# A long convolution with a gated MLP: how the input product of the first stage is laid out, evicted and loaded

## The chip, the core and the metric

The kernel runs on one core of a Trainium2 chip. The core's engines run programs of their own and wait for each other by semaphores: PE (TensorE) multiplies matrices out of on-chip memory (SBUF) into accumulators (PSUM), DVE (VectorE), ACT (ScalarE) and POOL (GpSimd) work element by element, and SP (SyncE) mostly issues DMAs. ACT and POOL can issue DMAs too. The metric is the device time of one execution in microseconds.

## What is computed

With S = 2048 positions and D = 640 channels (the reference, cut):

```python
def _A_ref(q, k, v, shift_k, ssm_k, ssm_D):
    k_pad = jnp.pad(k, ((0, 0), (ks - 1, 0), (0, 0)))          # ks = 4
    for t in range(ks):
        k_shift = k_shift + k_pad[:, t:t + S, :] * shift_k[:, ks - 1 - t][None, None, :]
    kv = k_shift * v
    # causal convolution of kv with ssm_k over 2048 positions, per channel, by FFT of length 2S
    y = irfft(rfft(kv) * rfft(ssm_k))[:S] + kv * ssm_D
    return q * y

mod = silu(c) @ w_mod                                           # six rows: sa, ca, ga, sb, cb, gb
h = layernorm(x) * (1 + ca) + sa                                # x = A_q
x = x + ga * _A_ref(h, A_k, A_v, A_shift_k, A_ssm_k, A_ssm_D)
h = layernorm(x) * (1 + cb) + sb
x = x + gb * (relu(h @ w1 + b1) ** 2 @ w2 + b2)                 # 640 -> 1728 -> 640
```

All inputs are fp32.

## The kernel before

The long convolution is done as a Fourier transform in two steps, both as products on PE. Position s is split as s = 64 n + i: n (32 values) lies on partitions, i (64 values) in the row. The channels are worked on in five blocks b of 128, and a block's channels stand as four groups a of 32 on partitions 32 a to 32 a + 31 (n inside). Blocks 1 and 2, and 3 and 4, share their loads (s is the number of such a load group: 0, 1, 2).

- *The short convolution* (`load_kv` L853, `kv` L874). A unit (s, u) holds 1024 elements on each partition: n = 32 or 16 values of i, by 32 or 64 channels. The tile `kt` has three rows more at its front, since the tap t looks back t positions. Of unit 0 these three rows are k's rows 61 to 63 of the partition before (position 64 n - 3 and on); eight small DMAs on ACT's queue fetch them, after POOL has cleared the three rows for the first partition of each group. Of later units ACT copies them. Then DVE, and for two of the four taps in groups 0 and 1 POOL, multiply `kt`, shifted by t, with the taps; DVE adds up in PSUM (`acc`, two banks) and multiplies with v into the tiles `px`. The taps lie in the channel's order, four to a channel, so that one tap's row steps 16 bytes. `px` is kept as (channel, i), so DVE writes it in steps of 256 bytes.
- *First step* (`unit_a` L906). For input (`px`, i = 0) and filter (`ph`, i = 1) of a block: each of a block's 32 channels of a group and each half of the partitions is a stationary matrix of 64 partitions by 64 columns, against the constants `cw` as the moving one; products for two halves e and two parts r go to the four quarters of the array. The profile counts two instructions for each fp32 product: 256 for one `px` or `ph`. ACT evicts 512 elements at a time to the tile `a` (`pac`): in pairs (d) before, the two elements of a pair 128 bytes apart in `a`.
- *Second step and back* (`spectra` L928, `front` L949, `back` L977, `unit_y` L1002): products of `a` with `gb`, the spectra's product on DVE and POOL (tiles `wx`), products with `gi` into `q` (evicted by ACT in runs of eight), transposes, products with `ca`, and the gate with the normalised q (tiles `up`). `early_h` (L943) does the filter's spectra of block 0 ahead. Besides there are the six rows of `mod` (products of `wm`) and the statistics of q's rows (BN_STATS on DVE).
- Then the MLP, 8 runs of 256 tokens over 14 slices of the hidden width, with weights split in two fp32r parts that stay in SBUF.

The names in the profile are those of the memory a tile lies in: `px` and `ph` are S0p or S1p (of block 0: `px` is S0p, `ph` is S1p), `kt`, v and the taps are KV, the tap products `up`, the sums `ps`, the tiles `m` are `wx`, and the spectra of `early_h` and the q tiles XP0p and XP1p.

The order of the work is not that of the code. Each operation is a node with an engine, a cost (`cost` L640) and its buffers; a planner (`order` L216) plays the engines against each other and takes on each the first ready node by the numbers in the table `URGE`, one for each node. What it gives out is a fixed order for each engine. An engine's queue is worked off strictly in that order. A DMA on SP also waits until the one `OUT` places ahead of it has landed (`sp_issue` L616). Most lines of the profile say L402, where `emit` issues all operations; so groups are told apart by their tiles.

Of the kernel before, what the change touches and what calls it, by code (L numbers as in the profile page):

```python
# [25 lines left out]
OUT = 4  # L26
# [87 lines left out]
class Graph:  # L114
# [101 lines left out]
    def order(self, lag=0.06, pelag=0.1, phase=0.0):  # L216
# [92 lines left out]
        dma_free, landed = 0.0, []  # L309
# [95 lines left out]
def _constants():  # L405
# [17 lines left out]
    for mm in range(1, 32):  # L423
# [32 lines left out]
        "cw": np.hstack([cw, gb[:, 0, 1, 0], gx]).astype(f),  # L456
# [7 lines left out]
def ssm_mlp_kernel(  # L464
# [37 lines left out]
    ident = sb.tile([P, P], F32, tag="ident", name="ident")  # L502
# [7 lines left out]
    cst = sb.tile([P, 256], F32, tag="cst", name="cst")  # L510
# [3 lines left out]
    ca = cst[:, 192:256]  # L514
    warm = sb.tile([P, 1], F32, tag="warm", name="warm")
    nc.scalar.dma_start(cst[:, 0:192], cw_d[:, 0:192])
# [123 lines left out]
    def cost(engine, op, args, kw):  # L640
# [7 lines left out]
        if engine == "DVE":  # L648
# [6 lines left out]
            return 0.17 + 0.001 * n if op != "scalar_tensor_tensor" else 0.17 + 0.00112 * n  # L655
# [168 lines left out]
    def load_gi(i):  # L824
# [6 lines left out]
        if i == 0:  # L831
            g.key = ("lgi", 0)
            sp_dma(gi[0:64, 1, 0].rearrange("p c n -> p (c n)"), cw_d[0:64, 192:320], 512)
# [6 lines left out]
    def load_taps(first):  # L840
        g.key = ("ltap", 0)
        if first:
            src = shift_k[:P].rearrange("(a c) t -> a (c t)", a=4)
            sp_dma(tapb[:, 0:128], src.unsqueeze(1).to_broadcast([4, 32, 128]), 512)
            return
        for s in range(2):
            src = shift_k[P + 256 * s : P + 256 * s + 256].rearrange("(a c) t -> a (c t)", a=4)
            sp_dma(tapb[:, 128 + 256 * s : 384 + 256 * s], src.unsqueeze(1).to_broadcast([4, 32, 256]), 1024)
# [4 lines left out]
    def load_kv(s, u):  # L853
# [20 lines left out]
    def kv(s, u):  # L874
# [3 lines left out]
        taps = tapb[:, at : at + 4 * w].rearrange("p (c t) -> p t c", t=4)  # L878
# [3 lines left out]
        for t in range(4):  # L882
            o = sbuf(f"ktmp_{s}_{u}_{t}", (P, n, w), TMP) if t else acc
# [808 lines left out]
```

## Time and profile before

| what | value |
|---|---|
| median of 3 runs | 739.98 us (738.59 to 777.24) |
| the profiled execution | 739.45 us |
| its span, first to last instruction | 737.7 us |
| mean granted TensorE clock | 0.974 |
| PE, share of the span | 646.3 us, 88% |
| weight loads, DVE, ACT, POOL | 574.6, 452.9, 337.4, 268.7 us |
| DMA | 62.47 MB in 108155 packets |

The span is 1.75 us shorter than the execution's own time. Weight loads (PEld) run beside PE's products. An engine's busy time is spread over stages that have different limits, so the stages are read one by one. In a row of waits stand the time in total, how often, and the longest.

### The profile page before, as it was taken

The numbers are of one execution on the slowest core, as the hardware profiler recorded it, in microseconds if no ns is written. First come the engines' busy times: TensorE is split into PE (matmuls) and PEld (weight loads), VectorE is DVE, ScalarE is ACT, GpSimd is POOL, SyncE is SP. The second block draws the span as 40 slices with busy tenths as digits, with TensorE's granted clock in tenths as the row PEclk, the third lists the DMA queues.
The fourth block names the chain that finished last, engine by engine and source line by source line (L and its number), as shares of the span: only waits on it lengthen the run. The fifth ranks groups of instructions, "written<-read, shape, count | busy, mean of one in ns | idle before, by whom it ended". The sixth has DMA issues, their size and how long they took to land.

```text
span 737.7 us, 17486 instructions
## 1 busy us (share of the span) xinstructions
PE 646.3 (88%) x7401; PEld 574.6 (78%) x7401; DVE 452.9 (61%) x754; ACT 337.4 (46%) x639; POOL 268.7 (36%) x259
## 2 busy tenths in 40 slices
PE   0048798978698989989999999999999999999996
PEld 0047575867577878849999988999999999999896
DVE  1798789789997736786526437446456365464432
ACT  1157256588768798655423424324324233243220
POOL 4647470666655765843311132102103004021001
PEclk9989999988889999998999999999999999999999
DMA  8698689979607521344201011002010020020011
GB/s 113 121 180 194 160 226 234 240 176 190 151 2 150 166 85 45 111 129 129 68 1 42 32 36 36 1 1 72 1 41 33 1 72 1 1 72 1 1 37 36
DMA packets 108155, 62.47 MB, mean 85 GB/s; under 512 B 78316, under 2 KB 98220, under 8 KB 108076
## 3 DMA queue, kind: packets, MB, share of 16 engines
q1 hardware_dynamic: 101884, 58.02, 33.3%
q10 hardware_dynamic: 5936, 3.32, 2.0%
q8 instruction: 58, 0.95, 0.6%
q14 instruction: 21, 0.17, 0.1%
q0 software_dynamic: 256, 0.00, 0.0%
HBM read 52.15 MB, written 9.18 MB: 83 GB/s over the span
## 4 chain that ended last, share of the span: by engine, by line
PE 74%; DVE 7%; DMA 7%; ACT 6%; issue 3%; POOL 3%; SPq 0%; ACTq 0%; DVEq 0%; POOLq 0%
PE ps L402 74%; ACT a L402 5%; DMA KV<-in_A_k_dram 2%; DVE up L402 2%; DMA KV<-in_A_v_dram 2%; DVE ps L402 1%; POOL up L402 1%; DVE wx L402 1%; DMA wm<-in_w_mod_dram 1%; DVE mtmp L402 1%; DMA gb<-in_gb_dram 1%; DMA S1p<-in_A_ssm_k_dram 1%; POOL wx L402 0%; SPq L617 0%; ACTq L402 0%
## 5 line engine op out<-in xcount | busy, mean ns | idle before, releaser
L402 PE MATMUL ps<-xt,w_S 128*128 128x256 f32 (+1 forms) x680 | 129.3, 331 | 0.0
L402 PEld LDWEIGHTS ps<-xt,w_S 128*128 128x128 f32 x680 | 104.8, 190 | 10.3 <-DVE xfs L402 0.2
L402 ACT ACTIVATE mtmp<-ps,b1t 128x256 f32<-128x256 f32 (+1 forms) x112 | 51.4, 473 | 113.7 <-PE ps L402 108.2
L402 PE MATMUL ps<-a,gb 128*64 128x128 f32 x1260 | 82.0, 281 | 8.7 <-DVE wx L402 5.1
L402 PEld LDWEIGHTS ps<-a,gb 128*64 128x64 f32 x1260 | 71.5, 140 | 22.5 <-DVE wx L402 7.4
L402 ACT ACTIVATE a<-ps 128x512 f32<-128x512 f32 x80 | 77.3, 1105 | 20.0 <-PE ps L402 19.7
L402 DVE TENSOR_TENSOR mtmp<-ps,mtmp 128x256 f32<-128x256 f32 (+1 forms) x99 | 41.1, 419 | 69.0 <-ACT mtmp L402 68.0
L402 PE MATMUL ps<-w_S,hring 128*128 128x320 f32 x456 | 78.0, 310 | 0.0
L402 POOL TENSOR_TENSOR wx<-wx 128x256 f32<-128x256 f32 x80 | 68.1, 872 | 20.0 <-DVE wx L402 19.7
L402 PEld LDWEIGHTS ps<-w_S,hring 128*128 128x128 f32 x456 | 70.1, 188 | 1.4
L402 DVE TENSOR_TENSOR hring<-mtmp,hring 128x256 fp32r<-128x256 f32 x74 | 36.3, 496 | 53.8 <-ACT hring L402 53.8
L402 PE MATMUL ps<-cst,S0p 64*64 64x64 f32 x1024 | 24.6, 255 | 50.3 <-DMA KV<-in_A_k_dram 43.2
L402 PEld LDWEIGHTS ps<-cst,S0p 64*64 64x64 f32 x1024 | 21.9, 165 | 55.4 <-DVE S0p L402 45.7
L402 ACT ACTIVATE hring<-mtmp 128x256 fp32r<-128x256 f32 x74 | 30.6, 416 | 67.9 <-PE ps L402 51.3
L402 POOL TENSOR_TENSOR x<-x,gb2row 128x640 f32<-128x640 f32 x16 | 25.3, 1594 | 90.6 <-ACT mtmp L402 90.6
L402 DVE TENSOR_TENSOR wx<-ps,wx 128x512 f32<-128x512 f32 x64 | 40.9, 685 | 22.8 <-PE ps L402 21.8
L402 POOL TENSOR_TENSOR x<-mtmp,x 128x640 f32<-128x640 f32 (+1 forms) x9 | 13.5, 1506 | 108.0 <-DVE mtmp L402 108.0
L402 POOL TENSOR_TENSOR up<-KV 128x1024 f32<-128x1024 f32 x12 | 38.0, 3188 | 27.7 <-DVE ps L402 16.6
L402 DVE TENSOR_TENSOR up<-KV 128x1024 f32<-128x1024 f32 x18 | 43.0, 2396 | 5.3 <-DMA KV<-in_A_k_dram 4.8
L402 DVE SCALAR_TENSOR_TENSOR mtmp<-mtmp 128x256 f32<-128x256 f32 x91 | 44.9, 500 | 1.8
L402 PE MATMUL ps<-gi,wx 64*128 64x128 f32 x640 | 41.5, 278 | 4.4 <-ACT q L402 2.0
L402 ACT ACTIVATE wx<-ps 128x512 f32<-128x512 f32 x49 | 29.5, 608 | 32.3 <-PE ps L402 29.1
(156 smaller groups left out, 1318.6 us busy)
## 6 DMA issues: line engine op xcount, KB each, us to landing
wm<-in_w_mod_dram SPq DMA_DIRECT2D x25, 320.0 KB, 4.1
KV<-in_A_k_dram SPq DMA_DIRECT2D x40, 128.0 KB, 3.7
KV<-in_A_v_dram SPq DMA_DIRECT2D x40, 128.0 KB, 4.5
S1p<-in_A_ssm_k_dram SPq DMA_DIRECT2D x20, 256.0 KB, 5.3
q<-in_A_q_dram SPq DMA_DIRECT2D x8, 640.0 KB, 4.3
out_dram<-x SPq DMA_DIRECT2D x14, 320.0 KB, 3.6
w1s<-in_B_w_dram SPq DMA_DIRECT2D x13, 320.0 KB, 3.4
w2s<-in_B_w_dram SPq DMA_DIRECT2D x13, 320.0 KB, 2.9
```

Of the source, the lines that this page charges most:

```text
L402: fn(*real, **{k: a.real() if isinstance(a, View) else a for k, a in kw.items()})
```

## The change

Six things, and a new table:

1. *Taps apart.* `load_taps` loads the taps into a staging tile and ACT copies them into four rows of neighbouring channels, one for each tap. The loads go row by row as before.
2. *Evictions in runs of eight.* `pac` goes through PSUM in steps of 64 elements, so that eight neighbouring elements of `a` are written one after the other.
3. *Last rows by a product.* k's rows 61 to 63 come by four plain DMAs a group into a tile of their own (`kend`). PE multiplies them with an identity shifted by one column (`step`), which moves each partition's rows to the next; ACT evicts them with a factor of 0 for the first partition of each group and 1 elsewhere (`later`, a new column of the constants).
4. *One queue.* These loads and the second half of the loads of q (`load_xp`) go to SP; ACT's queue keeps three at the start.
5. *`px` as k and v lie*: (i, channel) instead of (channel, i). DVE writes it in one run; PE's stationary columns are 128 bytes apart.
6. *`OUT` is 6 instead of 4*, and two costs in the planner change: the first DMA is assumed 2.5 us later, and operations of 1024 elements on DVE a little dearer. The tap products now take their buffers in the order of the program.

```diff
-OUT = 4
+OUT = 6
...
-        dma_free, landed = 0.0, []
+        dma_free, landed = 2.5, []
...
-    ident = sb.tile([P, P], F32, tag="ident", name="ident")
+    step = sb.tile([P, P + 1], F32, tag="ident", name="step")
+    ident, step = step[:, 1:], step[:, 0:P]
+    nc.vector.memset(step[:, 0:1], 0.0)
...
+        raw = sbuf(f"tap_{int(first)}", (P, D), [whole(f"STG{i}") for i in range(4)])
+        for s in (0,) if first else (1, 2):
+            at, w = (0, 128, 384)[s], WIDE[s]
+            src = shift_k[at : at + 4 * w].rearrange("(a c) t -> a (c t)", a=4)
+            sp_dma(raw[:, at : at + 4 * w], src.unsqueeze(1).to_broadcast([4, 32, 4 * w]), 16 * w)
+            copy(
+                act,
+                tapb[:, at : at + 4 * w].rearrange("p (t c) -> p c t", t=4),
+                raw[:, at : at + 4 * w].rearrange("p (c t) -> p c t", t=4),
+            )
...
         if u == 0:
-            pool.memset(kt[:, 0:3], 0.0)
-        else:
-            copy(act, kt[:, 0:3], KT[s, u - 1][:, n : n + 3])
+            end = sbuf(f"kend_{s}", (P, 3, w), [part(parent("XP1", 2560), 2048, ("XP1c",))])
         for a in (0, 2, 1, 3):
             cols = slice(BASE[s] + w * a, BASE[s] + w * a + w)
             if u == 0:
-                act_dma(kt[32 * a + 1 : 32 * a + 17, 0:3], kshift[0:16, 0:3, cols], 4 * w)
-                act_dma(kt[32 * a + 17 : 32 * a + 32, 0:3], kshift[16:31, 0:3, cols], 4 * w)
+                sp_dma(end[32 * a : 32 * a + 32], ksrc[:, 61:64, cols], 4 * w)
             sp_dma(kt[32 * a : 32 * a + 32, 3:], ksrc[:, n * u : n * u + n, cols], 4 * w)
+        if u == 0:
+            t = psum(f"kend_{s}", (P, 3, w), ANY)
+            with g.as_one(0.3):
+                mm(t.rearrange("p i c -> p (i c)"), step, end.rearrange("p i c -> p (i c)"), True, True)
+            act.activation(kt[:, 0:3], t, AF.Copy, scale=later)
+        else:
+            copy(act, kt[:, 0:3], KT[s, u - 1][:, n : n + 3])
...
-        taps = tapb[:, at : at + 4 * w].rearrange("p (c t) -> p t c", t=4)
+        taps = tapb[:, at : at + 4 * w].rearrange("p (t c) -> p t c", t=4)
...
-            mul(dve, px[b][:, :, n * u : n * u + n].rearrange("p g i -> p i g"), acc[:, :, c], vt[:, :, c])
+            mul(dve, px[b][:, n * u : n * u + n], acc[:, :, c], vt[:, :, c])
...
-                                (ph if i else px)[b][l, 8 * n + j, :],
+                                ph[b][l, 8 * n + j, :] if i else px[b][l, :, 8 * n + j],
...
-            o = AX[b][i].rearrange("p m (e d g) -> p m g e d", e=2, d=2)[:, :, 8 * n : 8 * n + 8, e]
-            copy(act, o, t[e].rearrange("p g m d -> p m g d"))
+            o = AX[b][i].rearrange("p m (e d g) -> p m e d g", e=2, d=2)[:, :, e, :, 8 * n : 8 * n + 8]
+            copy(act, o, t[e].rearrange("p g m d -> p m d g"))
...
-            (act_dma if h else sp_dma)(
-                t[64 * h : 64 * h + 64], qsrc[h, :, 4 * j : 4 * j + 4, BASE[s] : BASE[s] + w], 4 * w
-            )
+            sp_dma(t[64 * h : 64 * h + 64], qsrc[h, :, 4 * j : 4 * j + 4, BASE[s] : BASE[s] + w], 4 * w)
...
     URGE = {
-        ("b1", 0): [-1209, -1601],
```

The table `URGE` is new throughout, so every engine's order changes. Three places follow. The rows give the line, the operation, the tile written, the tiles read, and the shape; x2 means twice in a row.

The first loads on SP's queue. KV<-in_A_k_dram and KV<-in_A_v_dram are k and v, KV<-in_A_shift_k_dram the taps, XP1p<-in_A_k_dram the last rows, S1p<-in_A_ssm_k_dram the filter of block 0. Before:

```order
L617 DMA KV<-in_A_shift_k_dram 128x1x256
L617 DMA KV<-in_A_k_dram 32x32x32 x2
L617 DMA KV<-in_A_shift_k_dram 128x1x256
L617 DMA KV<-in_A_v_dram 32x32x32 x2
L617 DMA KV<-in_A_shift_k_dram 128x1x128
L617 DMA KV<-in_A_k_dram 32x32x32 x4
L617 DMA KV<-in_A_v_dram 32x32x32
L617 DMA KV<-in_A_k_dram 32x32x32
L617 DMA KV<-in_A_v_dram 32x32x32
L617 DMA KV<-in_A_k_dram 32x32x32
L617 DMA gb<-in_gb_dram 128x1024
L617 DMA KV<-in_A_v_dram 32x32x32 x3
```

Now:

```order
L621 DMA gb<-in_gb_dram 128x1024
L621 DMA KV<-in_A_k_dram 32x32x32 x3
L621 DMA XP1p<-in_A_k_dram 32x3x32
L621 DMA KV<-in_A_k_dram 32x32x32 x2
L621 DMA XP1p<-in_A_k_dram 32x3x32
L621 DMA KV<-in_A_k_dram 32x32x32 x2
L621 DMA tap_122<-in_A_shift_k_dram 128x1x128
L621 DMA KV<-in_A_v_dram 32x32x32
L621 DMA XP1p<-in_A_k_dram 32x3x32
L621 DMA KV<-in_A_k_dram 32x32x32
L621 DMA S1p<-in_A_ssm_k_dram 32x32x64
L621 DMA XP1p<-in_A_k_dram 32x3x32
```

The constants gb go first, the taps in the middle, and the filter's loads begin among those of k and v instead of behind them.

PE's first products. Before, the input's (S0p) come first and, after 128 of them, the filter's (S1p):

```order
L402 MATMUL ps_91<-cst,S0p 64x64 x2
L402 MATMUL ps_95<-cst,S0p 64x64 x2
L402 MATMUL ps_90<-cst,S1p 64x64 x2
L402 MATMUL ps_92<-cst,S1p 64x64 x2
L402 MATMUL ps_90<-cst,S1p 64x64 x2
```

Now the filter's 128 come first, then spectra of it (a, gb), and then, with the last rows of group 1 (XP1p, step) ahead, the input's:

```order
L402 MATMUL ps_94<-a_0_165,gb 64x128 x8
L402 MATMUL ps_92<-a_0_165,gb 64x128 x8
L402 MATMUL ps_93<-XP1p,step 128x192
L402 MATMUL ps_91<-a_0_165,gb 64x128 x8
L402 MATMUL ps_93<-cst,S0p 64x64 x2
L402 MATMUL ps_94<-cst,S0p 64x64 x2
```

The product with `step` waits for the loads of the last rows of group 1, which are SP's DMAs 30, 33, 37 and 40, and everything behind it on PE waits with it.

DVE's first work after the vector for `mod`. Before, the two units of group 0 follow each other:

```order
L402 TENSOR_TENSOR up_132<-KV 128x1024
L402 TENSOR_TENSOR ps_96<-KV 128x1024
L402 TENSOR_TENSOR ps_96<-ps_96,up_132 128x1024 x3
L402 TENSOR_TENSOR S0p<-ps_96,KV 128x32x32
L402 TENSOR_TENSOR ps_96<-KV 128x1024
L402 TENSOR_TENSOR up_132<-KV 128x1024
```

Now the statistics of the first q rows stand inside the second unit (four such pairs of rows, the first shown):

```order
L402 TENSOR_TENSOR ps_97<-KV 128x1024
L402 TENSOR_TENSOR up_142<-KV 128x1024
L402 TENSOR_TENSOR ps_97<-ps_97,up_142 128x1024 x3
L402 TENSOR_TENSOR S0p<-ps_97,KV 128x1024
L402 TENSOR_TENSOR up_142<-KV 128x1024
L402 BN_STATS s_217<-q_148 128x6 x2
L402 BN_AGGR st_238<-s_217 128x2
```

The product into S0p now writes one run of 1024 instead of a 32 by 32 pattern, and eight BN_STATS with four BN_AGGR stand ahead of the rest of the second unit.

More of the change, by code (lines that the diff above doesn't have):

```diff
@@ L509, in ssm_mlp_kernel @@
     nc.gpsimd.memset(dsm, 0.0)
-    cst = sb.tile([P, 256], F32, tag="cst", name="cst")
+    cst = sb.tile([P, 257], F32, tag="cst", name="cst")
     cw = cst[:, 0:128].rearrange("p (r n) -> p r n", r=2)
     gbx = cst[:, 128:192]
-    ca = cst[:, 192:256]
+    ca = cst[:, 193:257]
+    later = cst[:, 192:193]
     warm = sb.tile([P, 1], F32, tag="warm", name="warm")
-    nc.scalar.dma_start(cst[:, 0:192], cw_d[:, 0:192])
+    nc.scalar.dma_start(cst[:, 0:193], cw_d[:, 0:193])
     for a in range(4):
```

196 lines of the change are left out of this document (100 added, 96 removed), and 310 rows, old and new, of the table URGE.

## Prediction

> **What bounds the kernel now.** I read the slices of the page first, then a table by stage, then who PE (TensorE) waits for, then the groups of the early stages. In the slices each digit is a fortieth of the span, 18.4 us; PEclk is the granted TensorE clock.
>
> ```profile
> span 737.7 us, 17486 instructions
> ...
> PE   0048798978698989989999999999999999999996
> ...
> PEclk9989999988889999998999999999999999999999
> ```
>
> PE is idle for two slices, then broken up for some fifteen, then full to the end. The change touches only what stands ahead of the full part. The same by stage; the columns are the length, the busy time of PE, weight loads, DVE, ACT and POOL, then the clock, DMA share and GB/s.
>
> ```profile
> 0.00:12.00 12.00, 0.00 (x0) 0.00 (x0) 0.26 (x3) 2.98 (x4) 5.40 (x17) 1.00 0.59 90
> 12.00:24.00 12.00, 0.00 (x0) 0.00 (x0) 7.32 (x3) 2.04 (x3) 5.40 (x3) 1.00 1.28 175
> 0.00:43.25 43.25, 0.00 (x1) 0.00 (x1) 21.95 (x16) 6.88 (x10) 21.37 (x24) 1.00 0.80 130
> 43.25:72.30 29.05, 23.40 (x688) 21.67 (x688) 26.87 (x20) 21.60 (x27) 17.60 (x8) 0.88 0.95 188
> 72.30:150.00 77.70, 69.67 (x1124) 53.17 (x1122) 64.56 (x99) 38.73 (x59) 37.32 (x42) 0.98 0.83 213
> 150.00:226.00 76.00, 58.52 (x1280) 49.93 (x1280) 69.44 (x70) 58.56 (x104) 47.43 (x43) 0.87 0.63 126
> 226.00:329.50 103.50, 96.45 (x1746) 75.65 (x1746) 67.96 (x104) 78.75 (x138) 65.64 (x66) 1.00 0.42 117
> 329.50:737.70 408.20, 398.30 (x2567) 374.20 (x2567) 202.07 (x450) 132.90 (x303) 79.31 (x81) 0.99 0.11 32
> ```
>
> The MLP (from 329.5) is PE's: 398.3 of 408.2 us. Ahead of it there are four stages with different limits. Until 43.25 PE has nothing to do. From 43.25 to 72.3 it lacks 5.65 us (29.05 - 23.40), from 72.3 to 150 8.0, from 150 to 226 17.5, and from 226 on 7.05. The stage from 150 to 226 is the loose one: DVE is busy for 69.4 of 76 us, ACT for 58.6, and the clock is 0.87. What PE waits for between 43 and 331 us:
>
> ```profile
> PE ps L402 <- ACT a L402: 12.7, 18, 2.1
> PE ps L402 <- DVE wx L402: 8.5, 6, 3.3
> PE ps L402 <- POOL S1p L402: 4.2, 2, 3.1
> PE ps L402 <- DVE up L402: 4.0, 3, 1.8
> ...
> PE ps L402 <- DVE S0p L402: 2.1, 2, 1.9
> ```
>
> The largest is the eviction of the first stage (tile a), then work that stands behind DVE. So ACT's evictions and DVE's queue are the two things to price.
>
> **Evictions in runs of eight.** These are the groups that carry the sum (busy us, mean ns of one):
>
> ```profile
> L402 ACT ACTIVATE a<-ps 128x512 f32<-128x512 f32 x80 | 77.3, 1105 | 20.0 <-PE ps L402 19.7
> ...
> L402 DVE TENSOR_TENSOR up<-KV 128x1024 f32<-128x1024 f32 x18 | 43.0, 2396 | 5.3 <-DMA KV<-in_A_k_dram 4.8 <-issue 0.4
> ...
> L402 DVE TENSOR_TENSOR wx<-ps,wx 128x512 f32<-128x512 f32 x64 | 40.9, 685 | 22.8 <-PE ps L402 21.8 <-POOL wx L402 0.7 <-ACT wx L402 0.3
> ...
> L402 DVE TENSOR_TENSOR ps<-ps,up 128x1024 f32<-128x1024 f32 x30 | 36.9, 1231 | 7.2 <-POOL up L402 6.1
> ...
> L402 DVE TENSOR_TENSOR ps<-KV 128x1024 f32<-128x1024 f32 x10 | 27.3, 2728 | 0.1
> ...
> L402 ACT ACTIVATE q<-ps 128x512 f32<-128x512 f32 x39 | 21.6, 601 | 16.8 <-PE ps L402 15.9 <-ACT q L402 0.8
> ...
> L402 DVE TENSOR_TENSOR S0p<-ps,KV 128x512 f32<-128x512 f32 x12 | 12.2, 1057 | 2.2 <-DMA KV<-in_A_v_dram 2.1
> ...
> L402 DVE TENSOR_TENSOR S0p<-ps,KV 128x1024 f32<-128x1024 f32 x2 | 3.9, 1937 | 0.1
> ```
>
> The eviction to q already has the pattern that the one to a gets: runs of eight elements out, steps of 64 elements in PSUM, 512 elements. It takes 601 ns against 1105. I take 601, so ACT loses 80 x 0.504 = 40.3 us. Ends: the whole 40.3, or nothing if the PSUM side is what is slow (the q row speaks against that).
>
> **Taps apart.** Single instructions, or short rows of them, on DVE and on POOL (GpSimd):
>
> ```profile
> 33.50 1.97 DVE L402 TENSOR_TENSOR ps<-KV 128x1024 f32<-128x1024 f32 x1
> ```
> ```profile
> 163.64 1.28 DVE L402 TENSOR_TENSOR up<-up,row 128x512 f32<-128x512 f32 x2
> ```
> ```profile
> 18.54 4.64 DVE L402 TENSOR_TENSOR ps<-KV 128x1024 f32<-128x1024 f32 x1
> ```
> ```profile
> 16.67 4.67 POOL L402 TENSOR_TENSOR up<-KV 128x1024 f32<-128x1024 f32 x1 [3.94 <-DMA KV<-in_A_k_dram]
> ```
> ```profile
> 69.18 2.95 POOL L402 TENSOR_TENSOR up<-KV 128x1024 f32<-128x1024 f32 x1
> ```
> ```profile
> 72.32 3.46 POOL L402 TENSOR_TENSOR wx<-wx 128x256 f32<-128x256 f32 x5
> ```
>
> A tap product alone (taps 16 bytes apart) takes 1.97 us for 1024 elements. Two products of 512 with contiguous operands take 1.28, so 1024 take about 1.25: 0.72 less. DVE does 18 + 10 = 28 of them: 20 us. That they average 2.4 and 2.7 is another cost: the product at 18.54 took 4.64 us beside POOL's at 16.67, so the two block each other, and a shorter one blocks for less; I put nothing on that. The product with v goes from scattered to contiguous output: 16 x (1.06 - 0.685), with the tile wx as model, and 2 x (1.94 - 1.23) make 7.4 us. So DVE loses 27.5 us. POOL's 12 products take 2.95 us alone; its contiguous rows take 3.46 / 5 = 0.69 for 256 elements, 2.8 for 1024. So POOL gains nothing.
>
> **Last rows by a product, and one queue.** Twenty-four small DMAs leave ACT's queue, as do 12 loads of q, and three memsets leave POOL. Where they were late they held up DVE ahead of 43.25, which is reckoned anew below; behind it no row above names them, so I count no gain. SP gets 12 loads of k's last rows and the 12 of q, PE three products, ACT three scaled copies and three for the taps: about 1 us on the path. What is new is a wait: in PE's queue the product of the last rows of the second group stands ahead of the first input product (tile S0p), and it needs the fortieth DMA that SP issues. Sizes of the transfers:
>
> ```profile
> KV<-in_A_k_dram SPq DMA_DIRECT2D x40, 128.0 KB, 3.7
> ...
> S1p<-in_A_ssm_k_dram SPq DMA_DIRECT2D x20, 256.0 KB, 5.3
> ...
> gb<-in_gb_dram SPq DMA_DIRECT2D x2, 512.0 KB, 5.0
> ```
>
> **The start.** Before, PE starts with S0p, which waits for two whole units of DVE. Now it starts with S1p (the filter). Ahead of and with the fourth S1p load SP issues 3.52 MB: gb 0.52, k 1.05, last rows 0.05, taps 0.33, v 0.52, S1p 1.05. At 90 GB/s for 12 us and then 175 (first two stage rows) these land at 12 + 2.44 / 0.175 = 26 us; the first filter product follows, 17 us sooner. Up to the fortieth DMA come v 0.52, q 1.31, w_mod 0.33, gi 0.52, gb 0.52, k 0.39 and last rows 0.10 more, 7.2 MB in all: 12 + 6.15 / 0.175 = 47 us, and S0p cannot go on PE before. DVE is no later: it starts when k and the taps are in, near 16 us (1.8 MB by the same rates), and has four tap products, six sums, two products with v and q's first statistics to do until then. Rates of PE's products, and one row of DVE:
>
> ```profile
> 153.24 2.19 PE L402 MATMUL ps<-cst,S1p 64*64 64x64 f32 x128 [0.57 <-ACT wx L402]
> ```
> ```profile
> 252.34 4.59 PE L402 MATMUL ps<-a,gb 128*64 128x128 f32 x80
> ```
> ```profile
> L402 DVE BATCH_NORM_STATS2 s<-q 128x6 f32<-128x320 f32 x32 | 14.2, 475 | 0.4 <-DMA q<-in_A_q_dram 0.4
> ```
>
> The eight statistics moved ahead cost DVE 8 x 0.475 = 4 us; with 4 x 1.25 + 6 x 1.23 + 2 x 1.23 = 15 us that is 19, or 35 us from the start, and some 12 us of POOL's products may block it: covered by the 47, and gone as cover if the loads are faster. PE takes 17 ns for a small product, 57 for a large one. By 72.3 PE had done 512 small and 176 large. In the new order 256 small and 112 large stand ahead of S0p (11 us, done by about 40 with cold clock and waits). Behind it, up to the same total, 256 small and 64 large remain: 4.4 + 3.7 = 8 us, with a part at a low clock 10. That makes 57 against 72.3: **15 us** gained. Ends: 8 (loads no faster than 130 GB/s, the row up to 43.25) and 22 (six in flight reach the 213 of the row to 150).
>
> **The loose stages.** From 72.3 to 150 PE lacks only 8.0 us, and DVE loses 9 there (some eight products and eight with v): **5 us**, ends 0 and 10. (Less than the 9, since PE itself is nearly full.) From 150 to 226 alone:
>
> ```profile
> L402 ACT ACTIVATE a<-ps 128x512 f32<-128x512 f32 x24 | 23.5, 1103 | 2.8 <-PE ps L402 2.7
> ```
> ```profile
> L402 DVE TENSOR_TENSOR up<-KV 128x1024 f32<-128x1024 f32 x9 | 23.2, 2581 | 0.5 <-issue 0.4
> ...
> L402 DVE TENSOR_TENSOR ps<-KV 128x1024 f32<-128x1024 f32 x3 | 6.2, 2050 | 0.0
> ```
>
> Twelve tap products and six with v fall here: 12 x 0.72 + 6 x 0.38 = 11 us off DVE, and 24 evictions take 12 us off ACT. PE lacks 17.5 and loses up to 10 more by its clock (0.13 x 76). DVE is full there, so its 11 us count in full, and 2 for the clock: **13 us**, ends 5 and 24. From 226 on 24 evictions are left, and only waits for them go: **3 us**, ends 0 and 6. The MLP does not move.
>
> **Stationary columns at a stride.** The input's 1280 weight loads now read columns 128 bytes apart. No weight load of before does that over more than 8 bytes. The nearest row is the tap product: 1.97 for 1.25 where each element is 16 bytes from the last, a factor of 1.58. Were a small product wholly its load, 17 ns would become 27: 1280 x 10 = 13 us. But four quarters of the array work in turn, and part of the 17 ns is the product itself, so I take half, **6 us lost**; ends 0 and 22 (all doubled).
> SBUF — State Buffer (section Door 1: The DMA port swizzle, the note on cachelines) in the Trainium skill says that the memory's lines are 16 bytes, that each access to a new line pays, and that one may step four fp32 for free. It speaks against this part of the change. The trace agrees for DVE that new lines pay (1.97 against 1.25 us), though its taps are just four fp32 apart, which the page calls free. Taken in full for the weight loads, this is rival 2.
>
> **Sum.** On the profiled execution's 739.45 us (span 737.7; 0.5 under the median 739.98): 739.45 - 15 - 5 - 13 - 3 + 6 + 1 = 710 us.
>
> **Rivals.**
> 1. *Strided weight loads decide, and it is slower.* The gains are 36 us and the small costs 1, so at 35 / 1280 = 27 ns more on each input product nothing is left, and at 39 ns more (56 instead of 17) it is slower by 2%. If a load costs four times as much and the quarters don't overlap, it is 1280 x 51 = 65 us: 769. For it: no row shows such loads. Against: every strided row here costs less than twice.
> 2. *Strided loads cost their factor in full.* 13 us instead of 6: 717. For it: the tap row. Against: the quarters overlap, and PE has slack in the loose stage.
> 3. *Loads set the pace.* Until 226 us PE and DVE use 37 MB (130 x 43 + 188 x 29 + 213 x 78 + 126 x 76). If six in flight bring no more, the stages from 72.3 on gain 11 instead of 21: 720. For it: DMA shares of 0.95 and 0.83. Against: 0.63 in the loose stage.
> 4. *It unlocks more.* If PE runs nearly full from 26 us, the upper ends hold (22 + 10 + 24 + 6 = 62) and the stride costs 4: 739 - 62 + 5 = 682.
> 5. *The change does not do what it says.* Evictions stay at 1105 ns because reading PSUM in steps is what is slow: the start gains 8, the two stages behind it 5 each, the last none, and the stride costs 13: 739 - 18 + 14 = 735. For it: nothing but the risk; the q row is against it.
>
> **How the numbers follow.** Two per cent, about what a measurement of this kernel can tell from no change, is 725 to 755. Chances: the forecast (698 to 714) 0.40, rival 4 (below 698) 0.18, rival 2 (714 to 719) 0.12, rival 3 (719 to 725) 0.10, rival 5 and its like (725 to 755) 0.12, rival 1 0.08. So faster 0.80, same 0.12, slower 0.08. I leave out 0.07 at the fast end and 0.11 at the slow end: 685 to 728.
>
> **What would show it.** Groups: a<-ps near 600 ns; tap products near 1.3 us where POOL rests; the product with v near 0.69. The start: first S1p product near 26 us, first S0p product near 47 with PE waiting for k's last rows. Stride: 64 input products in more than 1.09 us (17 ns each). Xt, the MLP's first product, near 300 instead of 329.5. I am wrong if the input products take over 40 ns, if DVE waits for k or v again and again, or if the first MLP product comes at 320 or later.

## The result and the profile after

| kernel | median | against before on the same chip, 95% interval |
|---|---|---|
| before | 739.87 us | 1 |
| changed | 744.22 us (743.52 to 745.25, 4 runs) | 1.0066 (1.0045 to 1.0086) |

The changed kernel is 5 us slower (0.45 to 0.86 per cent); 710 was forecast. The ratio is of fast runs alone, and one run of before, of 777 us, was slow. The page of the changed kernel's profile shows PE starting a slice sooner and full no sooner:

```profile
span 742.8 us, 17442 instructions
...
PE   0298699877589999968999999999999999999996
...
PEclk9998899989899999987999999999999999999999
...
q8 instruction: 58, 0.95, 0.6%
```

By stretches (length, busy time of PE, weight loads, DVE, ACT, POOL, clock, DMA share, GB/s), cut where the first product of the transform (filter or input) and where the MLP's first product begin. Before, from 43.25 on (the stretch ahead of it stands in the prediction):

```profile
43.25:329.55 286.30, 248.04 (x4834) 200.46 (x4835) 228.88 (x290) 197.69 (x328) 168.05 (x156) 0.95 0.64 152
329.55:737.70 408.15, 398.30 (x2567) 374.17 (x2567) 202.02 (x450) 132.85 (x303) 79.27 (x81) 0.99 0.11 32
```

After:

```profile
0.00:28.90 28.90, 0.71 (x2) 0.50 (x2) 8.80 (x11) 7.41 (x11) 12.47 (x21) 1.00 1.02 152
28.90:336.96 308.06, 264.75 (x4840) 219.48 (x4841) 218.64 (x304) 172.49 (x339) 167.86 (x159) 0.94 0.67 152
336.96:742.80 405.84, 396.81 (x2565) 373.31 (x2565) 197.54 (x441) 128.64 (x296) 75.58 (x78) 0.99 0.10 28
```

Read as a ledger of spans: PE starts 14.4 us sooner. Then it is busy 16.7 us longer (264.75 - 248.04), and idle 5.1 longer (43.3 against 38.3). The MLP gives 2.3 back. That makes +5.1, with DVE 10 us and ACT 25 us less busy in the middle stretch. The groups after, and two of them before:

```profile
L402 ACT ACTIVATE a<-ps 128x512 f32<-128x512 f32 x80 | 42.6, 599 | 37.1 <-PE ps L402 37.1
...
L402 PE MATMUL ps<-cst,S0p 64*64 64x64 f32 x1024 | 35.3, 288 | 3.1 <-issue 3.1
...
L402 DVE TENSOR_TENSOR up<-KV 128x1024 f32<-128x1024 f32 x18 | 26.3, 1465 | 4.0 <-ACT KV L402 3.9
...
L402 DVE TENSOR_TENSOR ps<-KV 128x1024 f32<-128x1024 f32 x10 | 15.7, 1571 | 7.7 <-DMA KV<-in_A_k_dram 7.7
L402 DVE TENSOR_TENSOR S0p<-ps,KV 128x512 f32<-128x512 f32 x12 | 8.0, 685 | 2.4 <-PE ps L402 2.2
L402 DVE TENSOR_TENSOR xt<-xfs,xt 128x256 fp32r<-128x256 f32 x5 | 5.4, 1105 | 0.0
```

```profile
L402 PE MATMUL ps<-cst,S0p 64*64 64x64 f32 x1024 | 24.6, 255 | 50.3 <-DMA KV<-in_A_k_dram 43.2 <-ACT a L402 3.9 <-DVE S0p L402 2.1
L402 DVE TENSOR_TENSOR xt<-xfs,xt 128x256 fp32r<-128x256 f32 x5 | 3.1, 634 | 0.4 <-ACT xt L402 0.4
```

Evictions, taps and products with v came out as forecast or nearly so. The input products (S0p; 1024 of the 1280, one block lies elsewhere) cost PE 10.7 us more (35.3 against 24.6); the other 6 of the 16.7 are small rises in many groups, the largest that of the spectra's products (a, gb: 86.0 us against 82.0), at a granted clock of 0.94 against 0.95. What PE waits for from 20 us on (10.3 of POOL S1p is the wait at the start):

```profile
PE ps L402 <- issue: 13.1, 7, 4.4
PE ps L402 <- DVE wx L402: 12.1, 7, 5.1
PE ps L402 <- POOL S1p L402: 11.2, 2, 10.3
PE ps L402 <- ACT a L402: 4.5, 4, 2.2
PE ps L402 <- DVE xfs L402: 4.4, 1, 4.4
PE ps L402 <- ACT mtmp L402: 4.0, 2, 3.2
```

The wait for a fell from 12.7 to 4.5, as the evictions promised. New are 13.1 us of "issue" (2.2 before: PE waits for nothing that the profile shows), 3.6 more for wx, and 8.4 at the entry of the MLP. PE and then DVE there:

```profile
324.21 1.07 PE L402 MATMUL ps<-wx,cst 128*64 128x512 f32 x2
328.50 2.81 PE L402 MATMUL ps<-step,mtmp 128*128 128x128 f32 x11 [3.22 <-ACT mtmp L402]
332.10 0.47 PE L402 MATMUL ps<-step,mtmp 128*128 128x128 f32 x1 [0.79 <-ACT mtmp L402]
336.96 2.90 PE L402 MATMUL ps<-xt,w_S1a 128*128 128x256 f32 x12 [4.39 <-DVE xfs L402]
```

```profile
328.07 2.90 DVE L402 TENSOR_TENSOR w_S<-w2s,w_S 128x640 fp32r<-128x640 f32 x2
330.89 0.53 DVE L402 TENSOR_SCALAR xfs<-ps,cbs 128x256 f32<-128x256 f32 x1
331.34 1.54 DVE L402 TENSOR_TENSOR w_S<-w1s,w_S 128x640 fp32r<-128x640 f32 x2
332.81 3.43 DVE L402 TENSOR_TENSOR xt<-xfs,xt 128x256 fp32r<-128x256 f32 x2
336.27 0.54 DVE L402 TENSOR_SCALAR xfs<-ps,cbs 128x256 f32<-128x256 f32 x1
```

PE's last product of the convolution ends at 325.3, and PE comes to the MLP at 337 (before at 326.6 and 329.55). In the new order DVE's subtractions for weights stand ahead of xt, and xt takes 1.7 us each beside POOL's additions.

Three theories came of this. A: the strided columns double the product, and that ate the gains. B: six transfers in flight hold up PE's instructions (the issue waits). D: what ACT and DVE saved was never on the path.

### The profile page after: what moved, and what is told of

It is laid out like the page before. It is cut to its first block, busy times and chain, and to the rows that moved or that the text cites. A ratio compares the mean times of both kernels' runs of the same rounds, so it can differ in the third digit from the quotient of the medians.

```text
span 742.8 us, 17442 instructions
## 1 busy us (share of the span) xinstructions
PE 662.3 (89%) x7407; PEld 593.3 (80%) x7407; DVE 425.0 (57%) x755; ACT 308.5 (42%) x645; POOL 255.9 (34%) x256
## 4 chain that ended last, share of the span: by engine, by line
PE 80%; DVE 7%; DMA 6%; issue 3%; ACT 2%; SPq 1%; POOL 1%; DVEq 0%; POOLq 0%; ACTq 0%
PE ps L402 80%; DVE up L402 2%; DMA KV<-in_A_k_dram 2%; DVE wx L402 1%; DMA KV<-in_A_v_dram 1%; DMA S1p<-in_A_ssm_k_dram 1%; SPq L621 1%; DMA XP0p<-in_A_q_dram 1%; DVE ps L402 1%; DVE mtmp L402 1%; ACT a L402 1%; DMA XP1p<-in_A_k_dram 1%; ACT up L402 0%; DMA wm<-in_w_mod_dram 0%; DVE xt L402 0%
## 5 line engine op out<-in xcount | busy, mean ns | idle before, releaser
L402 PE MATMUL ps<-a,gb 128*64 128x128 f32 x1260 | 86.0, 288 | 14.5 <-DVE wx L402 7.9
L402 PEld LDWEIGHTS ps<-a,gb 128*64 128x64 f32 x1260 | 74.5, 144 | 27.2 <-DVE wx L402 10.8
L402 DVE TENSOR_TENSOR hring<-mtmp,hring 128x256 fp32r<-128x256 f32 x74 | 39.3, 540 | 64.9 <-ACT hring L402 61.3
L402 POOL TENSOR_TENSOR wx<-wx 128x256 f32<-128x256 f32 x80 | 64.2, 819 | 34.4 <-DVE wx L402 33.8
L402 ACT ACTIVATE a<-ps 128x512 f32<-128x512 f32 x80 | 42.6, 599 | 37.1 <-PE ps L402 37.1
L402 POOL TENSOR_TENSOR x<-mtmp,x 128x640 f32<-128x640 f32 (+1 forms) x9 | 13.1, 1464 | 123.9 <-DVE mtmp L402 123.9
L402 PE MATMUL ps<-cst,S1p 64*64 64x64 f32 x1536 | 32.4, 237 | 20.1 <-POOL S1p L402 11.2
L402 PEld LDWEIGHTS ps<-cst,S1p 64*64 64x64 f32 x1536 | 29.9, 154 | 22.8 <-POOL S1p L402 11.6
L402 PE MATMUL ps<-xt,w_S1a 128*128 128x256 f32 (+1 forms) x170 | 38.2, 343 | 6.0 <-DVE xfs L402 4.4
L402 PE MATMUL ps<-gi,wx 64*128 64x128 f32 x640 | 43.2, 286 | 0.1
L402 PEld LDWEIGHTS ps<-gi,wx 64*128 64x128 f32 x640 | 39.4, 195 | 4.6 <-issue 3.7
```

The lines of the kernel that those rows point to most:

```text
L402: fn(*real, **{k: a.real() if isinstance(a, View) else a for k, a in kw.items()})
```

## Experiments on the changed kernel

All ratios below are to runs of before on the same chip, with 95% intervals. One per cent is 7.4 us. Each trace shows one execution.

**The stride.** e1 undoes part 5, e9 stores px in pairs of channels, and e3 has another distance in each block (DVE's product with v and PE's stationary operand follow the layout; those lines are left out here):

```diff
-        px[b] = sbuf(f"px_{b}", (P, 64, DG), HALF[:3], line="px")
+        px[b] = sbuf(f"px_{b}", (P, DG, 64), HALF[:3], line="px")             # e1
+        px[b] = sbuf(f"px_{b}", (P, DG // 2, 64, 2), HALF[:3], line="px")     # e9
+        px[b] = sbuf(f"px_{b}", (P, DG // (1, 2, 4, 8, 16)[b], 64, (1, 2, 4, 8, 16)[b]), HALF[:3], line="px")     # e3
```

> The changed kernel with px laid out as before (channel, i), so that the stationary columns are neighbours again and DVE writes px in steps of 256 bytes; order unchanged. Theory A (the strided columns double the input product, 1280 x 15 to 17 ns = 19 to 22 us, and that is what ate the gains): 64 input products in 1.1 us again, 720 to 728 us. Rival D (what ACT and DVE saved was never on the path, and the stride isn't either): 738 to 746. Rival B (six DMAs in flight hold up PE's instructions): PE's waits put down to issue stay near 13 us, 735 to 742.

> The changed kernel with another layout of px in each block: stationary columns 4 bytes apart in block 0, 8 in block 1, 16 in block 2, 32 in block 3, 64 in block 4. It asks what the cost of a stride depends on: 64 input products take 1.1 us at 4 bytes and 2.1 to 2.2 at 128. If lines of 16 bytes decide: under 1.6 us at 8 bytes, 2.1 from 16 bytes on. If any step between columns costs the same: 2.1 at 8 bytes already. If the cost grows with the step: under 1.5 at 16 bytes. Time by theory A between the two layouts: 730 to 740 us.

> The changed kernel with px in pairs of channels (columns 8 bytes apart), nothing else. Theory F (PE's instructions are the floor under the input products): like the layout of before, 736 to 740 us, with PE's issue waits at 15 us or more, although DVE is 5 us shorter. Theory A (the stride is a cost in itself and DVE's v products are on the path): 722 to 733.

e1: 738.56 us, 1.0009 (0.9989 to 1.0028). e9: 737.82, 0.9988 (0.9963 to 1.0013). e3: 743.22, 1.0077 (1.0049 to 1.0104). Theory A falls in its size: with neighbouring columns the kernel gains 4 us (1.0066 - 1.0009), not 20. The products did get fast again, and the issue waits grew:

```profile
L402 PE MATMUL ps<-cst,S0p 64*64 64x64 f32 x1024 | 20.6, 226 | 7.3 <-issue 5.8 <-ACT a L402 1.2
```

```profile
PE ps L402 <- issue: 18.3, 10, 5.5
```

From 13.1 to 18.3 us: five of the fifteen that the products lost (35.3 to 20.6) came back as one kind of wait. Others went into products that took longer: the clock from the first filter product to the MLP is 0.92 in e1 and 0.94 in the change, and a, gb takes 88.0 us instead of 86.0. In e3 the stretches of block 0 (4 bytes), 1 (8), 2 (16), 3 (32) and 4 (64; its px lies in S1) read:

```profile
47.34 1.16 PE L402 MATMUL ps<-cst,S0p 64*64 64x64 f32 x64
...
106.73 0.71 PE L402 MATMUL ps<-cst,S0p 64*64 64x64 f32 x32
...
149.63 1.13 PE L402 MATMUL ps<-cst,S0p 64*64 64x64 f32 x32
...
223.71 2.17 PE L402 MATMUL ps<-cst,S0p 64*64 64x64 f32 x64
...
271.06 3.83 PE L402 MATMUL ps<-cst,S1p 64*64 64x64 f32 x128
```

At 8 bytes 32 take 0.71 us, as contiguous ones do; from 16 bytes on they take double (35, 34 and 30 ns each), and no more at 64 bytes than at 16. SBUF — State Buffer (section Door 1: The DMA port swizzle, the note on cachelines) in the Trainium skill asks for two hits on each 16-byte line; that agrees. Its figure of four fp32 stepped for free does not: 16 bytes cost the full double here.

**The products alone.** The issue waits point to the supply of instructions. PE has 14,814 instructions (7407 products, as many weight loads), and the queue "instruction" moved 0.95 MB in 58 packets: 16 KB each, one for 256 instructions, that is 128 products by the profile's count. Perfetto Trace Analysis (section The 4-stage abstract model) in the Trainium skill says that an instruction has 64 bytes; 256 of them are these 16 KB. A kernel of its own has PE do nothing else:

```diff
+    small("a", near, 1024)      # columns 4 bytes apart, no load
+    small("b", far, 1024)       # 128 bytes apart, no load
+    for flight, x, tag in ((4, near, "c"), (6, near, "d"), (6, far, "e")):
...
+        for i in range(40):
+            nc.sync.dma_start(ring[i % flight], rows[i % 16])
...
+        small(tag, x, 1024, gate=m)
```

> Not the kernel: PE alone does five stretches of 1024 input products (64 partitions x 64 columns, as in the first stage), each stretch behind some large ones; the output is not the reference's. Stretch a: columns 4 bytes apart, no load running; b: 128 bytes apart, no load; c: 4 bytes apart with four loads of 320 KB in flight; d: the same with six; e: 128 bytes apart with six. Theory F (new, since undoing the stride gained only some 6 us and PE's issue waits grew instead: PE's instructions arrive in blocks of 256, that is 128 products, and a block takes about 4 us alone, up to 7 beside loads, whatever the products cost): a and b both 28 to 34 us, c over 34, d over c, e like d. Theory A (the product itself is the limit): a, c and d 17 to 18 us, b and e 33 to 35.

The profile counts 2048 products for a stretch, twice what the expectation reckoned. Pieces of stretches a, b, c, d and e:

```profile
77.33 2.09 PE L40 MATMUL t<-cw,px 64*64 64x64 f32 x128 [1.64 <-issue]
81.05 2.09 PE L40 MATMUL t<-cw,px 64*64 64x64 f32 x128 [1.64 <-issue]
...
104.31 63.74 PE L40 MATMUL t<-cw,px 64*64 64x64 f32 x2048
...
197.27 2.09 PE L40 MATMUL t<-cw,px 64*64 64x64 f32 x128 [1.07 <-issue]
201.82 2.09 PE L40 MATMUL t<-cw,px 64*64 64x64 f32 x128 [2.46 <-issue]
...
261.79 3.39 PE L40 MATMUL t<-cw,px 64*64 64x64 f32 x128 [4.88 <-issue]
267.16 2.94 PE L40 MATMUL t<-cw,px 64*64 64x64 f32 x128 [1.98 <-issue]
...
339.55 4.15 PE L40 MATMUL t<-cw,px 64*64 64x64 f32 x128 [2.38 <-issue]
```

In stretch a the first 271 products run without a wait (4.19 us); from then on exactly 128 run (2.09 us, 16 ns each), then PE waits 1.4 to 1.9 us. From the piece at 46.40 to that at 95.42 lie 13 blocks: 3.77 us each, 29 ns a product. In stretch b nothing waits, and a product takes 31 ns (63.74 / 2048). So in a long row a strided product costs next to nothing more: it is hardly slower than instructions arrive. (The queue "instruction" moved 81 packets in this kernel, for its 20,800 instructions of PE: 256 each again.) With four loads in flight a block takes 4.6 us (six blocks from 183.34 to 211.19), with six 5.5 (five from 261.79 to 289.22), strided with six 5.0 (six from 339.55 to 369.70). Theory F: PE's instructions set a floor of about 29 ns a product in long rows, and 36 to 43 beside loads. That is one execution, with five or six blocks for each figure beside loads.

**Loads in flight.** e4 takes the changed kernel back to four at run time, e15 puts six into the kernel before:

```diff
-        if len(queued) > OUT:
+        if len(queued) > 4:         # e4; in e15 6, in the kernel before
```

> The changed kernel with four SP transfers in flight instead of six at run time, order unchanged. Rival B (the DMA load delays PE's instructions): PE's waits put down to issue fall from 13.1 us to under 4, 733 to 738 us. Theory A (the stride is the cause, the queue is not): the loads land later at the start, the first input product after 50 us, 744 to 752.

> The kernel before with six SP transfers in flight at run time, order unchanged. If loads set the pace at the start: the first product at 40 us or sooner instead of 43, 733 to 737. If loads delay PE's instructions (5.4 us for a block instead of 4.6, as in the products alone): issue waits from 2 to 6 us, 739 to 743.

e4: 745.38 us, 1.0102 (1.0081 to 1.0122); issue waits fell from 13.1 to 6.8 us, and nothing was gained: other waits grew by about as much (2.3 us for w_mod's loads, none in the change, 1.4 more for a, 1.1 for the filter, 0.9 for q). The first S0p came no later (48.15 us against 48.44). So theory B has its wait right and no gain to offer. e15: 741.86, 1.0047 (1.0024 to 1.0069): in the old order six in flight lose 3 us; where they lose it is not shown.

**Evictions and taps put back** in the changed kernel (in e11 ACT also copies the taps as they lie, a line left out here):

```diff
-            o = AX[b][i].rearrange("p m (e d g) -> p m e d g", e=2, d=2)[:, :, e, :, 8 * n : 8 * n + 8]
+            o = AX[b][i].rearrange("p m (e d g) -> p m g e d", e=2, d=2)[:, :, 8 * n : 8 * n + 8, e]   # e2
...
-        taps = tapb[:, at : at + 4 * w].rearrange("p (t c) -> p t c", t=4)
+        taps = tapb[:, at : at + 4 * w].rearrange("p (c t) -> p t c", t=4)                            # e11
```

> The changed kernel with the evictions to tile a in pairs as before (1.105 us instead of 0.6, 80 of them = 40 us more on ACT), all else unchanged. If the faster evictions are on the path (theory A counts some 13 us for them): PE's waits for a go from 4.5 back to 12 us or more, 752 to 760 us. Rival D (they never were): 743 to 746.

> The changed kernel with the taps in the channel's order again (16 bytes apart, tap products 0.5 to 0.7 us longer, 28 on DVE: some 15 to 20 us), order unchanged. If DVE is what PE waits for in the loose stage (as the prediction had it): PE's waits for wx grow from 12 to 20 us or more, 752 to 760. If PE's waits there are set by the order and by POOL's blocks: 744 to 748.

e2: 749.97 us, 1.0160 (1.0139 to 1.0182), the wait for a back at 14.7 us. e11: 750.61, 1.0168 (1.0143 to 1.0193), the wait for wx 19.7. Both came out between their two ranges. So each of the two is worth 7 us in the changed kernel, and theory D falls.

**The entry of the MLP.** e6 makes the subtractions for weights 7 and 8 and POOL's additions wait for xt, e8 is e6 with px in pairs, e16 moves only POOL's additions, with px in pairs:

```diff
+    xts = [n.id for n in g.nodes if n.key == ("xt", 0) and n.engine == "DVE"]
+    for n in g.nodes:
+        if n.key in (("wl", 7), ("wl", 8)) or (n.engine == "POOL" and n.key in (("f2", 0), ("f2", 1))):
+            n.deps.add(xts[-1])     # e6, e8
...
+    cut = [i for i, o in enumerate(plan) if o[2].key == ("mid", 0) and o[2].engine == "POOL"][5]
+    moved_on = [o for o in plan[:cut] if o[2].engine == "POOL" and o[2].key in (("f2", 0), ("f2", 1))]
+    plan = [o for o in plan[: cut + 1] if o not in moved_on] + moved_on + plan[cut + 1 :]   # e16
```

> The changed kernel with one edit: the four subtractions for weights 7 and 8 on DVE and POOL's four additions to x wait until the first tokens' xt is done; the order ahead of the MLP is unchanged. If the new order of the MLP's entry costs what the trace shows (PE waits 4.4 us for xfs behind DVE's subtractions, and xt takes 1.7 instead of 0.4 us beside POOL): first MLP product near 332 instead of 337, 738 to 741 us. If the MLP gives that back later (it is held by its weights): 743 to 745.

> The changed kernel with px in pairs of channels, columns 8 bytes apart (17 ns each, and DVE writes at 0.69 us per 512 elements, as block 1 showed), and the entry edit of e6. Sum of the two if they add up: 6 from the stride, 1 to 2 from DVE, 5 from the entry: 731 to 734 us, under the kernel before. If issue waits take it all (theory F in full): 737 to 740.

> The changed kernel with px in pairs, and POOL's four additions of the bias row to x moved behind its first six products of the MLP; every other queue as it was. If POOL's additions make DVE's subtractions into xt slow (1.7 instead of 0.4 us beside them, 3.4 us for two): the first MLP product 2 to 3 us sooner, 734 to 736 us. If not: 737 to 739 as with the pairs alone.

e6: 752.38 us, 1.0183 (1.0143 to 1.0224). The MLP's first product came at 333.0 instead of 337.0, but the later weights were then late in turn (PE waits 6.7 us for mtmp at 355.6), and it ends 8.6 us later than the change. e8: 747.02, 1.0103 (1.0064 to 1.0143), against 0.9988 for the pairs alone. e16: 740.36, 1.0004 (0.9977 to 1.0031): xt took 0.4 us each instead of 1.7, so it is POOL's additions that make it slow; the wait for xfs at the entry fell from 4.3 to 1.5 us, and the time did not. From its first product on the MLP then took longer: 416.6 us in e6 and 411.5 in e16, against 405.8 in the change and 405.6 in e9. All three ended above both of their ranges. What the entry costs in the end is not shown by these: the wait is there, but each cure moved it.

## Experiments on the kernel before, and the order alone

> The kernel before with part 2 alone: evictions in runs of eight, order unchanged. If ACT's evictions are on the path there (PE waits 12.7 us for a in 18 places): 729 to 734 us, waits for a under 6 us. Theory F (PE then waits for its instructions instead): issue waits grow from 2 to 8 us or more and it ends at 733 to 738. Rival D (never on the path): 737 to 741.

> The kernel before with part 5 alone: px as k and v lie, columns 128 bytes apart, order unchanged. Theory A (each product pays 15 ns on the path): 1280 x 15 = 19 us less what DVE saves (6), 750 to 756. Theory F (a product at 32 ns is only as slow as its instructions arrive, so most of it hides): 738 to 745.

> The kernel before with part 2 (evictions in runs of eight) and px in pairs of channels: the same order, loads of columns 8 bytes apart at 17 ns, DVE's products with v at 0.69 instead of 1.06 us. A candidate for the best version. If DVE's saving is on the path there (PE waits 8.3 us for wx): 729 to 733; if not: 734 to 736, as with the evictions alone.

> The kernel before with taps apart alone. e14 less e12 puts the taps at 11 us: 726 to 730. If they are worth that much only once the evictions are fast too: 732 to 737.

> The kernel before, in its own order of PE and POOL, with taps apart, evictions in runs of eight and px in pairs; loads, queues and four in flight as before. If DVE's taps are worth there what they are worth in the changed kernel (7.5 us): 727 to 731. If PE's wait for its instructions takes it: 733 to 736, with issue waits over 8 us.

The edits are those of the change, put into the kernel before with its order of PE and POOL left as it was; the lines of px and `pac` are those shown above the other way round, and the taps need places in the table:

```diff
-            o = AX[b][i].rearrange("p m (e d g) -> p m g e d", e=2, d=2)[:, :, 8 * n : 8 * n + 8, e]
+            o = AX[b][i].rearrange("p m (e d g) -> p m e d g", e=2, d=2)[:, :, e, :, 8 * n : 8 * n + 8]   # e7, e12, e14, e17
...
-        px[b] = sbuf(f"px_{b}", (P, DG, 64), HALF[:3], line="px")
+        px[b] = sbuf(f"px_{b}", (P, 64, DG), HALF[:3], line="px")             # e10, e17
+        px[b] = sbuf(f"px_{b}", (P, DG // 2, 64, 2), HALF[:3], line="px")     # e12, e14
...
+        ("ltapc", 0): [-5, -60, -70],     # e14, e17, e18: places for ACT's three copies of the taps
```

| run | in the kernel before | median | ratio, interval |
|---|---|---|---|
| e7 | evictions | 734.97 us | 0.9948 (0.9923 to 0.9973) |
| e10 | stride | 744.82 us | 1.0092 (1.0061 to 1.0123) |
| e12 | evictions, pairs | 735.59 us | 0.9956 (0.9934 to 0.9979) |
| e18 | taps | 729.55 us | 0.9890 (0.9864 to 0.9916) |
| e14 | evictions, taps, pairs | 724.11 us | 0.9812 (0.9782 to 0.9843) |

In the old order taps are worth 8 us, evictions 4, the three together 14 (e14 came out below both of its ranges). The products with v, which only e12 has beside e7, are worth nothing that can be seen. The stride alone costs 7 (with DVE's saving in it): in e10 PE is busy 15 us longer between its first product and the MLP (262.8 against 248.0), and 7 of them stand where it was idle before. e14 is the best version of all: 724 us.

Part of this is a sooner start. Before, PE's first input product (43.25 us) comes right behind DVE's second product with v, which ends at 43.20, though the profile puts the wait down to a load of k. With shorter tap products it comes at 39.0 us (e18), with shorter products with v at 42.0 or 42.3 (e12, e10), with both at 37.8 and 37.3 (e14, and e17 below); with the evictions alone it stays at 43.7 (e7). The row of e17:

```profile
37.33 2.94 PE L402 MATMUL ps<-cst,S0p 64*64 64x64 f32 x84 [37.33 <-DVE S0p L402]
```

These runs keep before's order on PE, so the time between two products can be compared product by product. By the traces e14 wins 5.5 us at the first product, loses 3.6 until the stage that began at 72.3, wins 2.8 in that stage, 7.9 in the one that began at 150, 0.3 in the last ahead of the MLP and 1.2 in the MLP: 14.

Last, the new order, queue, last rows and six in flight without parts 1, 2 and 5 (e13: the edits of e1, e2 and e11 together), and the three parts exactly as changed without these (e17):

> The changed kernel with parts 1, 2 and 5 undone (taps 16 bytes apart, evictions in pairs, px as before), so that the new order, the last rows by a product, the one queue and six in flight are left. By the single undone parts (evictions 7 us, taps 7.5, stride 6 the other way) 744 + 8.5 = 752 to 754: then the order and the queue lose 13 us or more against before although PE starts 14 us sooner. If the parts don't add up and the order is neutral: 738 to 745.

> The kernel before, in its own order and with its own loads, with the three parts as the change has them: taps apart, evictions in runs of eight, px as k and v lie (columns 128 bytes apart). With e14 (724) and a stride worth 5 to 6 us: 729 to 731. If in the old order the stride costs more once the other two are in (19 us in full): 740 or more; if nothing: 724 to 726. Against the changed kernel (744) it tells what order, queue, last rows and six in flight cost.

| | parts 1, 2, 5 out | parts 1, 2, 5 in |
|---|---|---|
| old order and loads | before: 1 | e17: 730.81 us, 0.9890 (0.9860 to 0.9919) |
| new order and loads | e13: 751.76 us, 1.0187 (1.0153 to 1.0220) | the change: 744.22 us, 1.0066 (1.0045 to 1.0086) |

By rows the parts gain 8 us in the old order and 9 in the new one (0.0121). By columns the new order and loads lose 14 without the parts and 13 with them (0.0176). They add up: the new order and loads, taken together, cost 13 to 14 us, and that is what turned a gain into a loss. Where e13 loses it, against before with the same layouts (the stretch from the first filter product to the MLP, then PE's waits from the first product of before on):

```profile
28.90:342.30 313.40, 251.56 (x4841) 203.02 (x4841) 251.59 (x306) 203.41 (x339) 181.69 (x159) 0.92 0.65 149
```

```profile
PE ps L402 <- ACT a L402: 17.3, 18, 3.9
PE ps L402 <- DVE wx L402: 16.6, 9, 6.2
PE ps L402 <- issue: 5.3, 6, 1.9
...
PE ps L402 <- DVE xfs L402: 4.3, 1, 4.3
PE ps L402 <- ACT mtmp L402: 4.0, 2, 3.2
```

PE is idle for 61.8 us there (313.40 - 251.56), before 38.3: 23.6 more. The start won 14.4. The idle time lies in the waits for a (12.7 before), wx (8.5), issue (2.2) and the entry (0.6 for mtmp). Another 3.5 us are busy time (251.6 against 248.0), at a clock of 0.92 against 0.95.

The change against e17, both with the three parts, shows the same: the first product is 8.4 us sooner (28.9 against 37.3), and on the way from there to the MLP PE is idle 14.7 us longer (43.3 against 28.6) and busy 6.7 longer (264.8 against 258.1, clock 0.94 against 0.96). The sums by rows agree, 8 and 9 us, but not the places. In e17 the way from the first product to the MLP is as long as before (286.7 against 286.3 us), and the gain lies at the start; in the new order the start does not wait for the taps.

## Why the prediction was wrong

**The failed step: the start.** "That makes 57 against 72.3: **15 us** gained" stood in the sum as a gain at the end. It failed twice.

First, the 57 did not come. It is the time by which 512 small and 176 large products are done. Two marks on the way were hit: the first filter product at 28.91 us (26 forecast) and the first S0p at 48.44 (47). But the second was luck. By the prediction PE is done by about 40 and then waits for the last rows' loads. PE did not wait for them: it came to their product at 46.90 without idling, because its own work had taken until then (3.5 us of it a wait for instructions). SP issued the fortieth DMA at 39.9, and loads of last rows took 3.2 to 4.9 us to land. Rows of PE:

```profile
37.64 0.80 PE L402 MATMUL ps<-cst,S1p 64*64 64x64 f32 x37 [3.50 <-issue]
...
46.90 0.59 PE L402 MATMUL ps<-XP1p,step 128*128 128x192 f32 x2
...
48.44 2.24 PE L402 MATMUL ps<-cst,S0p 64*64 64x64 f32 x64
...
51.63 6.42 PE L402 MATMUL ps<-cst,S0p 64*64 64x64 f32 x192
60.22 0.70 PE L402 MATMUL ps<-a,gb 128*64 128x128 f32 x4 [2.17 <-ACT a L402]
...
66.31 1.09 PE L402 MATMUL ps<-a,gb 128*64 128x128 f32 x16
```

With the last row the 176th large product is done, at 67.4; before it is at 72.4. That is 5 us, or 10 if one leaves out the eight products of wm (4.8 us) that the new table puts among them. Behind the first S0p 8 us, or 10 at a low clock, were reckoned; it took 19: the strided products 8.7 instead of 4.4, the products of wm, 2.2 of waiting, and a clock of 0.82 (0.91 ahead of it).

Second, the lead did not last. Counted by products, whatever their kind (so it is rough), PE is 11.4 us ahead of before at its 300th, 5.6 at its 688th, 8.5 at its 2000th, 0.9 at its 3500th and not at all at its 4700th (305.4 us against 305.3). A lead is worth something at the end only if what PE waits for later comes sooner as well. It did not: PE waits longer for DVE's and ACT's tiles in the middle, and at the entry. Order, queue, last rows and six in flight, forecast at -15 + 1, measured +13 to +14 (e13, and the change against e17). That is 27 of the 34 us by which the forecast missed.

**The other parts, -21 + 6 = -15, measured -8 (e17).** Mechanisms right, sizes off:
- Evictions: 599 ns as forecast (601), 4 to 7 us on the path.
- Taps: 1.47 and 1.57 us instead of 1.25, and 7 to 8 us on the path, of which in the old order some 4 at the start (e18). POOL's tap products, put at no gain, went from 2.9 to 2.35 us where they run alone (38.0 to 30.3 for the twelve).
- Products with v: 0.69 as forecast, worth nothing at the end (e12 against e7).
- The loose stages' 5 + 13 + 3 = 21 came to 2.8 + 7.9 + 0.3 = 11 (e14), half; the rest of e14's 14 lies at the start and in the MLP. That DVE's "11 us count in full" was wrong: they don't even where DVE stands in PE's waits. PE then waits for other things, for its instructions above all (e14 has 6.4 us of issue, before 2.2).
- The stride: 6 forecast, 4 to 7 measured (e1, e10, e14 against e17). The size was right by luck, the reason wrong: the product doubled, which was the upper end of 22, and of the 12 to 15 us that PE is busy longer 5 to 7 hid where it had been idle (e1, e10, e14 against e17), in e1 and e14 mostly in waits for its instructions. "Half" had nothing to do with it.

**"The MLP does not move."** It takes 405.84 instead of 408.15 us, but its entry takes 11.7 us from PE's last product ahead of it (325.3) instead of 3: the new table put other work ahead of xt. Whether that is a net loss stays open (e6, e16). The first product of the MLP, forecast near 300, came at 337; 320 was the prediction's own sign of being wrong.

**The rivals.** Rival 1 (strided loads decide) had the sign right and the cause wrong. Rival 2 (strided loads cost their factor in full) had the products nearer, 14 to 18 ns more instead of 10, and their price too high, 4 to 7 us instead of 13. Rival 3 (loads set the pace) is not settled: more in flight gained nothing (e4, e15), and in e17 PE waits 7.4 us for w_mod's loads (0.8 before), but in the changed kernel no wait of PE behind the first filter product names a load. Rival 4 (PE nearly full from 26 us) did not come: PE is idle for 43 us between 28.9 and the MLP. Rival 5 fell with the first row of groups. The case that came about, a new order that costs more than it wins, was not among them, though the change replaced every number of the table.

**What stays open.** Which of the moves in the new order make the waits for wx and a longer; the order was not run apart from the one queue and the last rows by a product. And what six in flight are worth in the new order (e4 and the change have touching intervals).

## What to carry to other kernels

Take a diff apart into what makes instructions cheaper and what reorders them, and price the order by itself: here three cheap edits gain 8 to 14 us in the old order (e17, e14), and the order and loads that came with them lose 13. An earlier start is not a gain at the end unless the tiles that PE waits for later come earlier too; follow them to the last wait. (In e17 a start 5.9 us sooner is still there at the end: there DVE and ACT had become faster as well, and the order was the old one.) In long rows of small products look at the supply of instructions before their cost: waits put down to "issue" every 128 products mean that cheaper products, or cheaper neighbours, gain little.

## What the hardware showed that was not expected

- PE's instructions come 256 at a time: a row of small fp32 products went no faster than one block of 128 in 3.77 us with no loads, 4.6 with four loads of 320 KB in flight, 5.5 with six (e5).
- Stationary columns 8 bytes apart load as fast as neighbouring ones (32 products in 0.71 us); from 16 bytes on a product takes 30 to 35 ns instead of 17, and 128 bytes are no worse than 16 (e3, e5).
- Writing px in runs of two fp32 costs DVE nothing: 0.68 us for 512 elements (e14), as in one run (0.685), against 1.06 in single elements. So a layout in pairs serves both engines.
